# K and V loaded by quarters of the channels, and PSUM banks shared between matmuls and transposes, in a fused feed-forward and FFT-convolution kernel

## Chip, cores and metric

One core of one Trainium2 chip. The metric is the device time of one execution in microseconds (us); lower is better. A run is told with its median, lowest and highest time.

## The reference, cut to what matters

Forward and backward pass of a layer that multiplies a state-space convolution with a gated feed-forward network. B=1, S=2048 tokens, D=512 channels, F=1376, all bfloat16.

```python
def _A_ref(q, k, v, shift_k, ssm_k, ssm_D):
    k_pad = jnp.pad(k, ((0, 0), (ks - 1, 0), (0, 0)))             # ks = 4
    for t in range(ks):
        k_shift = k_shift + k_pad[:, t:t + S, :] * shift_k[:, ks - 1 - t][None, None, :]
    kv = k_shift * v
    # ... y = irfft(rfft(kv, 2S) * rfft(ssm_k, 2S))[:S], along the tokens
    y = y + kv * ssm_D[None, None, :]
    return q * y

xn = _layernorm(x)                                                # x = A_q
s  = _A_ref(xn, A_k, A_v, A_shift_k, A_ssm_k, A_ssm_D)
g  = silu((sigmoid(xn @ w_gate) * (xn @ w_up)) @ w_down)
out = x + s * g
# and jax.vjp of all this: gradients of q, k, v, shift_k, ssm_k, ssm_D and the three weights
```

## The kernel before

The kernel doesn't issue instructions as its code is run. A recorder notes every operation; a list scheduler then orders each engine's instructions by a cost model and gives each PSUM tile a bank when its first writer is placed. So all instructions carry the line of one helper (L519 here; a few lines more in kernels with code added above it), and a change of one table reorders all engines. On the chip each engine works in that fixed order and waits for semaphores.

The change touches only the first stage, the **FFT stage**, some 168 of 549 us. Four streams are woven into each other there: ten feed-forward tiles (`strG`), the transforms of the filter (`strK`), the shift convolution and the transforms of K*V (`strV`), and the products and inverse transforms (`strX`). Each of the last three goes through four quarters (`cg`) of 128 channels.

PSUM has eight banks. In the FFT stage a matmul tile takes a pair of them, a transpose tile one:

```python
KINDS = {"mm2": [(0, 1), (2, 3), (4, 5)], "mm2c": [(0, 1), (2, 3)], "mm1": [(0,), (1,), (2,), (3,)],
         "acc": [(4,), (5,)], "tr": [(6,), (7,)]}
```

K and V come in halves of 256 channels, into single buffers, on SyncE's queue. The sum of the convolution, `acc`, has a single buffer as well, and so have the filter's quarter `KT` and its spectrum `KFg`:

```python
kh_r = Ring(ar, [NJ + 3, 2 * GW])          # GW = 128 channels, NJ = 16 blocks of 128 tokens
vg_r = Ring(ar, [NJ, 2 * GW])
acc_r, term_r, kvt_r = Ring(ar, [NJ, GW]), Ring(ar, [NJ, GW]), Ring(ar, [NJ, GW])   # shortened
KFg_r = Ring(ar, [4, 1024])

def ld_k(cp):
    kh = kh_r.next()
    nc.gpsimd.memset(kh[0:1, 0:3, :], 0.0)
    nc.sync.dma_start(kh[:, 3:, :], kC[:, :, c0:c1])
    ld_halo(nc.sync, kh[:, 0:3, :], kHalo[:, 0:3, c0:c1])

def strV():                                # VectorE, quarter by quarter
    for cg in range(NG):
        acc = acc_r.next()
        for lag in (3, 2, 1, 0):           # acc = k*shift (lag 3), then term = k*shift, acc = acc + term
            ...
        nc.gpsimd.dma_start(ksh_d[cg], acc.rearrange("p j d -> p (j d)"))   # store, for the backward pass
        nc.vector.tensor_tensor(kvt, acc, vg[:, :, lc:lc + GW], ALU.mult)
        if cg == 1:
            ld_k(1); ld_v(1)               # the second half, when the single buffer is free
        ...

def strX():                                # KFg = spectrum of the filter, stored too
        for qq in range(4):
            yield from step3(QfK, qq, X_RI, KFg[:, qq])
            nc.gpsimd.dma_start(KK_d[cg, qq, :, 0], KFg[:, qq])
```

## Time and profile before

| | before |
|---|---|
| time | 550.47 us (549.67 to 550.48, 3 runs) |
| profiled span | 548.7 us |
| TensorE, VectorE, ScalarE, GpSimd busy | 526.4, 458.2, 350.6, 140.9 us |
| TensorE busy from 140 to 170 us | 27.46 of 30 us |

How to read it. A row of busy times by stage gives the stretch, its length, the busy time of TensorE, of its weight loads, of VectorE, ScalarE and GpSimd with the number of instructions, then the granted TensorE clock, the mean busy share of the 16 DMA engines, and GB/s. A timeline row gives start, length, engine, line, operation, and in brackets the idle time before it with what ended it. PE is TensorE, DVE VectorE, ACT ScalarE, POOL GpSimd, and SPq SyncE's queue, where a row's length is that of the issue and not of the transfer. A row of waits gives who waited for whom, us in total, times, longest. The lines of the kernel before that carry the argument stand in the prediction.

### The profile page before, as it was taken

How to read it: one execution, taken by the hardware profiler on the slowest of the kernel's cores; microseconds unless marked ns; L12 is line 12 of the kernel's file. 1: busy time of each engine (PE TensorE's matmuls, PEld its weight loads, DVE VectorE, ACT ScalarE, POOL GpSimd, SP SyncE). 2: the span in 40 equal slices, each digit the busy share in tenths (PEclk: the TensorE clock that was granted, in tenths of full speed). 3: DMA queues.
4: the chain of work that ended last, by engine and by line, in shares of the span. 5: the costliest groups of instructions: out<-in, count | busy, mean ns of one | idle time of the engine just before them, and what ended most of it. 6: DMA issues, size and time to landing. Idle time of an engine off the chain costs nothing.

```text
span 548.7 us, 13419 instructions
## 1 busy us (share of the span) xinstructions
PE 526.4 (96%) x5517; PEld 373.2 (68%) x5517; DVE 458.2 (84%) x831; ACT 350.6 (64%) x461; POOL 140.9 (26%) x250
## 2 busy tenths in 40 slices
PE   3999899999989999999999999999999999999996
PEld 2998798898768566677775666655666665665644
DVE  9599999956876999898989998929969999999650
ACT  7888999977985334444443345438868876966411
POOL 3225324203212222213122210221141033141221
PEclk9999999999999999999999999999999999999999
DMA  8878799857434798989999999999585469787441
GB/s 287 243 200 255 263 274 267 238 170 206 140 116 103 215 196 223 243 198 212 200 264 141 290 248 325 296 298 283 155 292 158 159 206 353 242 267 239 133 132 46
DMA packets 125287, 120.35 MB, mean 219 GB/s; under 512 B 74963, under 2 KB 104489, under 8 KB 125226
## 3 DMA queue, kind: packets, MB, share of 16 engines
q1 hardware_dynamic: 109946, 71.22, 51.9%
q0 software_dynamic: 14752, 48.27, 27.4%
q8 instruction: 43, 0.70, 0.5%
q14 instruction: 18, 0.15, 0.1%
q10 hardware_dynamic: 528, 0.00, 0.0%
HBM read 54.23 MB, written 47.55 MB: 185 GB/s over the span
## 4 chain that ended last, share of the span: by engine, by line
PE 72%; DVE 14%; issue 8%; ACT 5%; POOL 1%; POOLq 0%; ACTq 0%
PE psum L519 72%; DVE slab L519 14%; ACT slab L519 5%; POOL out_dram L519 1%; POOL slab L519 0%; POOLq L1455 0%; POOLq L519 0%; ACTq L519 0%; POOLq L1444 0%
## 5 line engine op out<-in xcount | busy, mean ns | idle before, releaser
L519 PE MATMUL psum<-slab 128*128 128x128 bf16 (+4 forms) x5517 | 526.4, 258 | 17.9 <-ACT slab L519 10.9
L519 PEld LDWEIGHTS <-slab 128*128 128x128 bf16 (+2 forms) x5517 | 373.2, 102 | 170.7 <-issue 18.7
L519 DVE TENSOR_TENSOR slab<-slab 128x512 bf16<-128x512 bf16 (+7 forms) x467 | 299.6, 683 | 7.9 <-ACT slab L519 3.0
L519 ACT CAST slab<-psum 128x1024 bf16<-128x1024 f32 (+3 forms) x252 | 207.2, 862 | 74.5 <-PE psum L519 65.9
L519 ACT COPY slab<-psum 128x1024 bf16<-128x1024 bf16 (+2 forms) x94 | 80.4, 877 | 90.1 <-PE psum L519 88.5
L519 POOL DMA_DIRECT2D out_dram<-slab x75 | 44.2, 590 | 206.8 <-ACT slab L519 111.2
L519 DVE TENSOR_TENSOR slab<-psum,slab 128x512 bf16<-128x512 f32 (+3 forms) x84 | 63.8, 760 | 23.2 <-PE psum L519 12.6
L519 ACT ACTIVATE slab<-slab 128x512 bf16<-128x512 bf16 (+3 forms) x48 | 38.6, 807 | 16.9 <-DVE slab L519 16.3
L519 ACT ACTIVATE slab<-psum 128x512 bf16<-128x512 f32 (+1 forms) x64 | 37.2, 583 | 11.5 <-PE psum L519 9.8
L519 DVE SCALAR_TENSOR_TENSOR slab<-slab 128x1 f32<-128x1 f32 (+3 forms) x64 | 27.9, 436 | 12.5 <-ACT slab L519 11.7
L519 POOL DMA_DIRECT2D KK_d<-slab x32 | 17.4, 545 | 54.7 <-ACT slab L519 43.9
L519 DVE CAST slab<-psum 128x1024 bf16<-128x1024 f32 (+1 forms) x21 | 25.1, 1196 | 5.6 <-PE psum L519 5.3
L519 POOL DMA_DIRECT2D slab<-in_A_q_dram x29 | 16.0, 552 | 30.4 <-DMA out_dram<-slab 14.9
L519 DVE COPY slab<-psum 128x1024 bf16<-128x1024 bf16 (+2 forms) x22 | 13.5, 622 | 10.9 <-PE psum L519 8.6
L519 DVE TENSOR_SCALAR slab<-slab 128x1 f32<-128x1 f32 (+7 forms) x70 | 19.5, 313 | 0.2
L519 DVE SCALAR_TENSOR_TENSOR slab<-psum,slab 128x512 f32<-128x512 f32 x16 | 11.0, 685 | 7.3 <-PE psum L519 7.2
L519 POOL TENSOR_TENSOR slab<-slab 128x1 f32<-128x1 f32 x16 | 11.5, 716 | 20.3 <-DVE slab L519 20.1
L519 POOL DMA_DIRECT2D slab<-in_grad_out_dram x16 | 8.9, 559 | 26.2 <-DMA out_dram<-slab 14.7
L519 DVE BATCH_NORM_STATS2 slab<-slab 128x6 f32<-128x512 bf16 x16 | 10.9, 681 | 0.0
L519 POOL DMA_DIRECT2D slab<-in_A_k_dram x12 | 10.1, 845 | 1.7 <-PE psum L519 1.4
L519 POOL MEMSET slab<- 1x384 bf16 (+4 forms) x14 | 5.7, 417 | 12.9 <-DVE slab L519 12.5
L519 POOL DMA_DIRECT2D slab<-slab x8 | 4.5, 567 | 10.2 <-issue 9.5
(21 smaller groups left out, 38.2 us busy)
## 6 DMA issues: line engine op xcount, KB each, us to landing
KK_d<-slab POOLq DMA_DIRECT2D x32, 256.0 KB, 3.8
slab<-KK_d SPq DMA_DIRECT2D x16, 512.0 KB, 5.6
out_dram<-slab POOLq DMA_DIRECT2D x58, 128.0 KB, 4.3
hS_d<-slab SPq DMA_DIRECT2D x16, 352.0 KB, 3.0
dgS_d<-slab SPq DMA_DIRECT2D x16, 352.0 KB, 3.4
duS_d<-slab SPq DMA_DIRECT2D x16, 352.0 KB, 4.4
slab<-hS_d SPq DMA_DIRECT2D x8, 512.0 KB, 4.8
slab<-dgS_d SPq DMA_DIRECT2D x8, 512.0 KB, 4.9
```

What stands on the lines that cost most here:

```text
L519: getattr(getattr(self.nc, eng), meth)(*[place(v) for v in a], **{x: place(v) for x, v in k.items()})
```

## The change

The intent: TensorE, 96% busy, waits now and then for the bank that its next tile needs. Matmul tiles get a fourth pair, and transposes four banks, both out of the same eight. K and V come by quarters, so that two slots let the next quarter arrive while one is worked on, and they start behind the gate weights. Their queue is GpSimd's, so that they don't block SyncE's.

```diff
-    KINDS = {"mm2": [(0, 1), (2, 3), (4, 5)], "mm2c": ...
-             "acc": [(4,), (5,)], "tr": [(6,), (7,)]}
+    KINDS = {"mm2": [(0, 1), (2, 3), (4, 5), (6, 7)], "trA": [(6,), (7,), (4,), (5,)], "mm2c": ...
+             "acc": [(4,), (5,)], "tr": [(6,), (7,)]}
...
-    PS["mm"], PS["wide"] = "mm2", True
+    PS["mm"], PS["tr"], PS["wide"] = "mm2", "trA", True
...
-    kh_r = Ring(ar, [NJ + 3, 2 * GW])
-    vg_r = Ring(ar, [NJ, 2 * GW])
+    kh_r = Ring(ar, [NJ + 3, GW], n=2)
+    vg_r = Ring(ar, [NJ, GW], n=2)
...
+    def ld_kv(cg, after=None):
+        c0, c1 = cg * GW, (cg + 1) * GW
+        kh, vg = stA["kh", cg], stA["vg", cg] = kh_r.next(), vg_r.next()
         nc.gpsimd.memset(kh[0:1, 0:3, :], 0.0)
-        nc.sync.dma_start(kh[:, 3:, :], kC[:, :, c0:c1])
+        if after is not None:                                   # holds the load back
+            nc.vector.tensor_copy(kh[0:1, 3, 0:1], after)
+            nc.vector.tensor_copy(vg[0:1, 0, 0:1], after)
+        nc.gpsimd.dma_start(kh[:, 3:, :], kC[:, :, c0:c1])
         ld_halo(nc.sync, kh[:, 0:3, :], kHalo[:, 0:3, c0:c1])
+        nc.gpsimd.dma_start(vg, vC[:, :, c0:c1])
...
-    ld_k(0)
-    ld_v(0)
+    ld_kv(0, wg[0:1, 2, 0:1])
+    ld_kv(1, wg[0:1, 2, 0:1])
...
-            if cg == 1:
-                ld_k(1)
-                ld_v(1)
+            if cg + 2 < NG:
+                ld_kv(cg + 2)
```

Cut: `ld_v`, which goes; the indices that follow from the quarters; and the return to two transpose banks after the stage.

More of the change, by code (lines that the diff above doesn't have):

```diff
@@ L188 @@
     ENGS = ("tensor", "vector", "scalar", "gpsimd", "sync")
-    KINDS = {"mm2": [(0, 1), (2, 3), (4, 5)], "mm2c": [(0, 1), (2, 3)], "mm1": [(0,), (1,), (2,), (3,)],
+    KINDS = {"mm2": [(0, 1), (2, 3), (4, 5), (6, 7)], "trA": [(6,), (7,), (4,), (5,)], "mm2c": [(0, 1), (2, 3)], "mm1": [(0,), (1,), (2,), (3,)],
              "acc": [(4,), (5,)], "tr": [(6,), (7,)]}
@@ L645, in ps_tr @@
     def ps_tr(shape, dt=bf16, name=None):
-        return nc.ps("tr", shape, dt)
+        return nc.ps(PS["tr"], shape, dt)
     ident = Ring(ar, [P]).ap
@@ L787, in ld_halo @@
         eng.dma_start(dst[113:128], src[112:127])
-    def ld_k(cp):
-        c0, c1 = cp * 256, (cp + 1) * 256
-        kh = kh_r.next()
+    def ld_kv(cg, after=None):
+        c0, c1 = cg * GW, (cg + 1) * GW
+        kh, vg = stA["kh", cg], stA["vg", cg] = kh_r.next(), vg_r.next()
         nc.gpsimd.memset(kh[0:1, 0:3, :], 0.0)
-        nc.sync.dma_start(kh[:, 3:, :], kC[:, :, c0:c1])
+        if after is not None:
+            nc.vector.tensor_copy(kh[0:1, 3, 0:1], after)
+            nc.vector.tensor_copy(vg[0:1, 0, 0:1], after)
+        nc.gpsimd.dma_start(kh[:, 3:, :], kC[:, :, c0:c1])
         ld_halo(nc.sync, kh[:, 0:3, :], kHalo[:, 0:3, c0:c1])
-        stA["kh", cp] = kh
-    def ld_v(cp):
-        vg = vg_r.next()
-        nc.sync.dma_start(vg, vC[:, :, cp * 256:(cp + 1) * 256])
-        stA["vg", cp] = vg
+        nc.gpsimd.dma_start(vg, vC[:, :, c0:c1])
     stS_r.append(Ring(ar, [FP]))
@@ L940, in strV @@
         for cg in range(NG):
-            kh, vg = stA["kh", cg // 2], stA["vg", cg // 2]
-            lc = (cg % 2) * GW
+            kh, vg = stA.pop(("kh", cg)), stA.pop(("vg", cg))
             c0, c1 = cg * GW, (cg + 1) * GW
@@ L945, in strV @@
             for lag in (3, 2, 1, 0):
-                src = kh[:, 3 - lag: 3 - lag + NJ, lc:lc + GW]
+                src = kh[:, 3 - lag: 3 - lag + NJ, :]
                 skl = skb[:, lag:lag + 1, c0:c1].to_broadcast([P, NJ, GW])
@@ L957, in strV @@
             kvt = kvt_r.next()
-            nc.vector.tensor_tensor(kvt, acc, vg[:, :, lc:lc + GW], ALU.mult)
-            if cg == 1:
-                ld_k(1)
-                ld_v(1)
+            nc.vector.tensor_tensor(kvt, acc, vg, ALU.mult)
+            if cg + 2 < NG:
+                ld_kv(cg + 2)
             yield 1024
@@ L1005, in kernel_impl @@
         r.free()
-    PS["mm"], PS["wide"] = "mm1", False
+    PS["mm"], PS["tr"], PS["wide"] = "mm1", "tr", False
     zw = {k: Ring(ar, [D], at=kv_off["kh"] + 1024 * q) for q, k in enumerate(("sigz", "gate", "s_out", "dgate", "t2"))}
```

## The prediction

> **What bounds the kernel now.** I read the page first, then the busy times by stage, then TensorE's waits and its timeline in the first 170 us (the FFT stage, which is all that the change touches), then SyncE's own timeline.
>
> The page's list of busy times, then busy time by stage (stretch, length, busy us of each engine, clock, DMA share, GB/s):
>
> ```profile
> PE 526.4 (96%) x5517; PEld 373.2 (68%) x5517; DVE 458.2 (84%) x831; ACT 350.6 (64%) x461; POOL 140.9 (26%) x250
> ...
> 0.00:15.00 15.00, 6.42 (x44) 4.75 (x45) 13.98 (x55) 11.92 (x13) 4.47 (x16) 1.00 0.85 288
> 15.00:30.00 15.00, 15.00 (x242) 14.95 (x241) 8.49 (x22) 11.70 (x17) 3.37 (x6) 1.00 0.91 225
> 30.00:110.00 80.00, 75.07 (x1118) 66.82 (x1116) 77.12 (x119) 74.38 (x94) 29.98 (x51) 1.00 0.84 251
> 110.00:140.00 30.00, 29.67 (x444) 26.42 (x442) 19.70 (x25) 23.70 (x31) 6.43 (x12) 1.00 0.62 177
> 140.00:170.00 30.00, 27.46 (x361) 22.39 (x359) 22.84 (x31) 25.80 (x30) 7.00 (x13) 1.00 0.36 118
> 170.00:549.00 379.00, 372.76 (x3323) 237.83 (x3320) 316.04 (x583) 203.11 (x281) 89.64 (x152) 1.00 0.83 221
> ```
>
> The whole is bound by TensorE: 96% busy, and its work is not changed. So the change can only give back TensorE's idle time. That is 15 - 6.4 = 8.6 us in the first 15 us, 155 - 147.2 = 7.8 us from 15 to 170 us, and 379 - 372.8 = 6.2 us in 379 us after that. From 30 to 110 us VectorE (77.1 of 80) and ScalarE (74.4 of 80), which empty PSUM, are as full as TensorE. There is little to win there by buffers alone.
>
> TensorE's waits from 0 to 170 us (us in total, times, longest), then its timeline at the start and at the end of that stage (start, length; idle before in brackets):
>
> ```profile
> PE psum L519 <- ACT slab L519: 10.0, 16, 4.2
> PE psum L519 <- DVE slab L519: 3.0, 5, 1.9
> PE psum L519 <- DMA slab<-in_A_shift_k_dram: 2.2, 1, 2.2
> ```
>
> ```profile
> 8.28 1.89 PE L519 MATMUL psum<-slab 128*128 128x128 bf16 x16 [4.18 <-ACT slab L519]
> 12.09 1.86 PE L519 MATMUL psum<-slab 128*128 128x128 bf16 x16 [1.92 <-DVE slab L519]
> 14.20 22.78 PE L519 MATMUL psum<-slab 128*128 128x128 bf16 x368 [0.25 <-ACT slab L519]
> ...
> 157.32 3.97 PE L519 MATMUL psum<-slab 128*128 128x128 bf16 x52 [0.46 <-DVE slab L519]
> 162.41 5.27 PE L519 MATMUL psum<-slab 128*128 128x512 bf16 x59 [1.12 <-ACT slab L519]
> 168.08 2.11 PE L519 MATMUL psum<-slab 128*128 128x128 bf16 x35 [0.40 <-ACT slab L519]
> ```
>
> No wait of TensorE after 2.2 us is for a DMA. All are for an engine that empties PSUM or makes an operand. A matmul is shown 0.22 us long though the next starts 0.0555 us after it, so short stalls hide in the busy time. Taking starts instead (step to the next matmul less 0.0555 us, or less 0.214 us for 512 columns, where more than 0.05 us is over), I count 13.7 us of stalls from 15 to 170 us. When I follow the kernel's built order, in nearly every one the operand had long been there, and the matmul came just after the eviction of the tile that held its PSUM bank before. With 2.7 us such in the first 15 us, bank waits make 16.4 us.
>
> SyncE's timeline, the loads of K (512-byte runs), V and the filter:
>
> ```profile
> 5.59 8.41 SPq L519 DMA_DIRECT2D slab<-in_A_k_dram  x2
> 14.04 0.55 SPq L519 DMA_DIRECT2D slab<-in_A_v_dram  x1
> 14.72 3.64 SPq L519 DMA_DIRECT2D slab<-in_A_ssm_k_dram  x1
> ...
> 60.44 0.57 SPq L519 DMA_DIRECT2D slab<-in_A_k_dram  x1
> 64.30 0.56 SPq L519 DMA_DIRECT2D slab<-in_A_v_dram  x1
> ```
>
> K blocks the queue from 5.6 to 14.0 us, but the weights were issued ahead of it and land by 13.5 us; the filter's second quarter lands only at 24.8 us. The second half of K and V is asked for at 60 us, when its single buffer is free, and lands at 66.9 and 75.6 us; TensorE uses it at 96.8 us. Nobody waits for it.
>
> **What the Trainium skill says.** "Perfetto Trace Analysis", Optimization Strategy: the same gap repeating on the engine that should be saturated can mean there isn't enough PSUM for the next tile. The 21 waits above agree. "TensorE: Matmul & The Clock Gate", Part 1: a cold array starts 128-column matmuls every 107 ns, a warm one every 56 ns. Here the 16 transposes at 12.09 us come 107 ns apart, and those after about 18 us 55.5 ns, so work that starts earlier also warms the array earlier. "DMA: Bandwidth & Descriptors", Issuing engines are not separate DMA queues: moving a load to GpSimd saves the issuing queue's time only. The same page, Specifications, wants 512 bytes or more per run; the quarters have 256. A K quarter of this form, loaded by GpSimd at 408.87 us late in this trace, landed 5.3 us after its issue with 1.2 us of issue. That is slower per byte, but no disaster.
>
> **The change part by part.**
>
> *PSUM.* In the FFT stage matmuls may use four bank pairs, not three; transposes four single banks, not two. The number of banks stays eight, so this is flexibility, not capacity. The order of the changed kernel can be read before it runs. For each PSUM tile I added up the TensorE work (0.0555 or 0.214 us each) between the last matmul of the bank's former tile and its own first, and summed what falls short of 1.3 us (an eviction of 1024 columns takes 1.0 us on ScalarE, 1.2 on VectorE, plus a matmul's 0.2). Before: 15.0 us, after 11.5. That is an index, not a time, but the 15.0 stand against 16.4 us measured, so -3.5 of index is some -3.8 us. By place: first 8 us of TensorE work 3.9 to 5.0; to 24 us 0.8 to 0.1; 24 to 95 us 8.3 to 8.4; the last 42 us 5.5 to 2.9. So the gain should be at the end of the stage, some 2 us, and hardly any (I put 0.7, for the earlier start of what follows) where VectorE and ScalarE are full.
>
> *The head.* At 12.09 us the first filter transposes waited 1.92 us for a bank that VectorE emptied late. Their operand was ready at 10.44 us. With four transpose banks they start near 10.6 us, are 107 ns apart, and one of the two evictions moves from ScalarE to VectorE; so the first FFT matmuls, at 14.58 us before, come at about 13.3 us: -1.3 us. The index rises there because later work moves up behind it.
>
> *K and V.* Four tiny copies of about 0.15 us on VectorE, 0.6 us in the first 13 us, hold K and V back until half of the gate weights has landed (9.6 us before), which is earlier than VectorE gets to the copies: no wait. GpSimd issues four loads of 1.2 us from about 12.4 to 17.2 us. At some 2.5 us of data each they should be in by 27 us; the shift convolution began at 31.55 us. The filter quarter now goes from SyncE at about 12.5 us and lands near 17-20 us instead of 24.8; its transposes are placed about 10 us of TensorE work earlier, at roughly 20 us. Worth by itself: nothing, 0 to -0.5 us, as no wait was for K or V.
>
> Sum: -1.3 - 0.7 - 2.0 = -4.0 us; 550.5 - 4.0 = 546.5 us.
>
> **Rivals.** (1) *VectorE and ScalarE are the true bound of the stage.* For it: 96 and 93% from 30 to 110 us, 22.8 and 25.8 of 30 from 140 to 170 us. Then a freed bank only moves the wait and all that remains is the head: 548.5 to 549.5 us. (2) *New waits from the loads.* The filter's transposes now stand before the end of the first feed-forward tile; if the filter shares the DMA engines with 2 MB of short runs and lands after 20 us, TensorE waits for it in order. Also a layer-norm step on GpSimd stands behind the four issues, until about 17.5 us, used near 20 us. Either could cost 1 to 4 us: 548 to 552 us. (3) *Sharing hurts:* one transpose in bank 6 or 4 blocks a whole pair. The built order has this in it, and the index doesn't rise past the head. (4) *More than counted:* all 16.4 us of bank waits can't go, since evictions take their time; half of them would be 542 us.
>
> **Range and chances.** Middle 546.5; (4) sets the low end at 542.5, (1) and (2) the high end at 550.0. For 2% faster (539.5) nearly all recorded idle time of the stage except the start would have to go: 4%. For 2% slower, 11 us of new waits: 2%. Within 2%: 94%.
>
> **What would show it.** Right: TensorE's second group of transposes starts near 10.6 us and the long unbroken group near 13; idle from 15 to 170 us falls from 7.8 to some 5-6 us, mostly after 140 us; busy times of all engines stay; no TensorE wait for a DMA after 15 us; after 170 us the same 6 us idle. Wrong: a wait of TensorE or VectorE for K, V or the filter between 15 and 45 us; idle unchanged after 140 us (rival 1); or a change after 170 us, where I expect none.

## More of the kernel before

A finished feed-forward tile is transposed by the DMA, from SBUF to SBUF, and then stored; both go through SyncE's queue:

```python
nc.sync.dma_start_transpose(st.rearrange("p (a b) -> p a b", b=128), srcT.rearrange("p a t -> p (a t)"))
...
nc.sync.dma_start(dst, st)                 # hS_d
```

One more view matters later: SyncE's own timeline of the kernel before, around the DMA transpose of the second feed-forward tile.

```profile
40.01 1.43 SPq L519 DMA_TRANSPOSE slab<-slab  x1
44.04 0.34 SPq L519 DMA_DIRECT2D hS_d<-slab  x1
```

The store of the transposed tile goes out 4 us after the transpose, as soon as that is done. In the same stretch the store of the first convolution's sum (`ksh_d`) landed 6.1 us after its issue at 42.9 us.

## The result, and the profile after

The changed kernel took 548.12 us (547.8 to 548.75, 4 runs) beside 550.24 us of the kernel before in the same rounds: a ratio of 0.9964 [0.9947, 0.9982]. Ratios in this document are the mean time of one kernel's fast runs over that of the other's of the same rounds, with a 95% interval, so not quite the ratio of the medians quoted. Executions over 1.5% slower than the fastest of the same kernel are left out of the means. The kernel was run once more, in another session, beside three experiments:

> The changed kernel once more, unaltered, beside the three that follow, on their chip. Expected: 547.5 to 549.0 us, 0.995 to 0.9975 of the kernel before, mean clock 1.0 in the profiled run. If it comes out at 1.000 or above, the gain of 2 us measured first was a matter of one session and there is nothing to explain.

It gave 548.15 us (548.02 to 548.78), ratio 0.9967 [0.9953, 0.9980]. The 2 us are real, and half of the 4 us foretold. The trace of this second session is complete (the first lacks 59 matmul records) and is used from here on; where both have a step, they agree within 0.1 us. Its page's line of busy times and its busy time by stage:

```profile
PE 524.3 (96%) x5517; PEld 371.5 (68%) x5517; DVE 457.3 (84%) x841; ACT 347.1 (63%) x455; POOL 150.6 (28%) x260
...
0.00:15.00 15.00, 7.81 (x67) 5.90 (x68) 13.73 (x58) 12.30 (x13) 6.73 (x19) 1.00 0.84 278
15.00:30.00 15.00, 13.47 (x229) 13.10 (x227) 9.38 (x28) 12.29 (x17) 7.96 (x11) 1.00 1.07 256
30.00:110.00 80.00, 73.04 (x1089) 64.96 (x1087) 75.15 (x114) 70.46 (x88) 32.45 (x54) 1.00 0.90 242
110.00:140.00 30.00, 29.64 (x436) 26.03 (x434) 20.47 (x28) 23.55 (x28) 6.78 (x13) 1.00 0.67 189
140.00:170.00 30.00, 29.41 (x412) 24.88 (x412) 24.72 (x42) 26.76 (x34) 7.84 (x15) 1.00 0.41 135
```

TensorE gains 1.4 us of busy time in the first 15 us (6.42 to 7.81) and 1.95 us in the last stretch (27.46 to 29.41). It loses 1.5 us from 15 to 30 us and 2.0 us from 30 to 110 us, where the prediction saw a small gain. TensorE's timeline at the start, and GpSimd's:

```profile
10.51 3.90 PE L519 MATMUL psum<-slab 128*128 128x128 bf16 x44 [0.29 <-DVE slab L519]
14.84 1.09 PE L519 MATMUL psum<-slab 128*128 128x128 bf16 x16 [0.43 <-ACT slab L519]
16.24 3.45 PE L519 MATMUL psum<-slab 128*128 128x128 bf16 x59 [0.31 <-ACT slab L519]
20.17 1.63 PE L519 MATMUL psum<-slab 128*128 128x128 bf16 x25 [0.47 <-ACT slab L519]
22.55 2.66 PE L519 MATMUL psum<-slab 128*128 128x128 bf16 x43 [0.75 <-ACT slab L519]
```

```profile
12.74 1.20 POOL L519 DMA_DIRECT2D slab<-in_A_k_dram  x1
13.93 2.27 POOL L519 DMA_DIRECT2D slab<-in_A_v_dram  x1
16.19 1.15 POOL L519 DMA_DIRECT2D slab<-in_A_k_dram  x1
17.33 1.15 POOL L519 DMA_DIRECT2D slab<-in_A_v_dram  x1
18.50 0.57 POOL L519 TENSOR_TENSOR slab<-slab 128x1 f32<-128x1 f32 x1
```

The 1.9 us wait at 12.09 us is gone; the transposes start at 10.51 us. But a step of a layer norm on GpSimd (18.50 us) now stands behind the four issues, and VectorE waits 2.4 us for it. That is passed on to ScalarE and comes back to TensorE as the waits at 20.17 and 22.55 us.

**The lead.** To see where time is won or lost, I counted TensorE's work in its built order (each matmul at the distance of back-to-back starts, 0.0557 us, or 0.2147 us for 512 columns) and compared when each kernel had done the same amount. Negative: ahead of the kernel before, in us, at the moment when that one stood at the time in the head row.

| kernel | 25 us | 61 us | 93 us | 142 us | 199 us |
|---|---|---|---|---|---|
| changed kernel | -0.5 | -2.7 | +2.1 | +1.6 | -2.5 |
| banks alone | -2.0 | -2.3 | +4.8 | +5.0 | +1.6 |
| loads alone | -0.8 | -0.3 | -0.1 | +0.6 | +1.0 |
| second half's loads late | -0.5 | -2.6 | +5.9 | +6.0 | +2.6 |
| second quarter later | -2.2 | 0.0 | +3.9 | +3.3 | -0.8 |
| changed, two sums | -0.6 | -2.8 | +1.2 | +0.8 | -3.3 |
| second quarter later, two sums | -2.2 | -4.3 | +2.5 | +2.0 | -2.1 |
| banks alone, two sums | -1.8 | -3.7 | +2.6 | +2.9 | -0.6 |
| second quarter later, plain copies | -2.2 | -4.3 | -0.1 | -0.6 | -4.7 |
| pairs shared, transposes in two banks | -0.8 | -1.5 | +1.4 | +1.4 | -0.5 |

The kernels are those of the experiments below. From 199 us to 297 us, the last point compared, the curves are flat: the rest of the program only starts earlier or later (only the one with the second half's loads late loses 3.2 us more). The profiled spans differ by 1.7 us (548.7 and 547.0) where the lead is 2.5 us; where the other 0.8 us goes was not followed (at 540 us the lead is still 2.3 us, so most of it goes at the very end). The changed kernel's tale is: 2.4 us ahead at 16 us, 1.9 given back, 2.2 more won by 61 us, 4.7 lost by 93 us, 4.1 won after 142 us.

### The profile page after: what moved, and what is told of

It is laid out like the page before. It is cut to its first block, busy times and chain, and to the rows that moved or that the text cites. A ratio compares the mean times of both kernels' runs of the same rounds, so it can differ in the third digit from the quotient of the medians.

```text
span 546.9 us, 13392 instructions
## 1 busy us (share of the span) xinstructions
PE 520.3 (95%) x5458; PEld 371.5 (68%) x5517; DVE 457.2 (84%) x841; ACT 347.1 (63%) x455; POOL 151.0 (28%) x260
## 4 chain that ended last, share of the span: by engine, by line
PE 66%; DVE 16%; issue 8%; ACT 5%; POOL 2%; DMA 1%; POOLq 0%; DVEq 0%; ACTq 0%
PE psum L519 66%; DVE slab L519 16%; ACT slab L519 5%; DMA ksh_d<-slab 1%; POOL out_dram L519 1%; POOL slab L519 1%; ACT L519 0%; POOLq L1451 0%; POOL KK_d L519 0%; POOLq L519 0%; DVEq L519 0%; ACTq L519 0%; POOLq L1440 0%
## 5 line engine op out<-in xcount | busy, mean ns | idle before, releaser
L519 PE MATMUL psum<-slab 128*128 128x128 bf16 (+3 forms) x5458 | 520.3, 256 | 21.7 <-ACT slab L519 11.5
L519 ACT CAST slab<-psum 128x1024 bf16<-128x1024 f32 (+4 forms) x260 | 214.2, 866 | 80.2 <-PE psum L519 72.4
L519 ACT COPY slab<-psum 128x1024 bf16<-128x1024 bf16 (+2 forms) x82 | 68.5, 861 | 85.5 <-PE psum L519 85.2
L519 ACT ACTIVATE slab<-slab 128x512 bf16<-128x512 bf16 (+3 forms) x46 | 36.8, 805 | 18.4 <-DVE slab L519 17.8
L519 DVE COPY slab<-psum 128x1024 bf16<-128x1024 bf16 (+2 forms) x34 | 21.0, 636 | 8.1 <-PE psum L519 7.8
L519 DVE CAST slab<-psum 128x1024 bf16<-128x1024 f32 (+1 forms) x13 | 14.8, 1141 | 4.7 <-PE psum L519 4.5
L519 POOL DMA_DIRECT2D slab<-in_A_k_dram x16 | 14.9, 930 | 7.1 <-DVE slab L519 3.9
L519 POOL TENSOR_TENSOR slab<-slab 128x1 f32<-128x1 f32 x16 | 10.6, 663 | 13.6 <-DVE slab L519 13.3
L519 POOL DMA_DIRECT2D slab<-sF_d x7 | 3.8, 537 | 22.7 <-DVE slab L519 18.5
L519 POOL MEMSET slab<- 1x384 bf16 (+3 forms) x16 | 5.9, 376 | 14.5 <-DVE slab L519 11.3
```

Of the source, the lines that this page charges most:

```text
L519: getattr(getattr(self.nc, eng), meth)(*[place(v) for v in a], **{x: place(v) for x, v in k.items()})
```

## The experiments

Each diff below is against the changed kernel unless said otherwise. Results were correct except where "wrong" stands.

### 1. The banks alone, and the loads alone

The first kernel has only the changes of `KINDS` and `PS`, the second only those of the loads.

> The kernel before with the PSUM part of the change alone (four bank pairs for matmuls, four single banks for transposes; K and V as before). Theory A (the gain is the banks', and the new loads cost in the middle of the stage, because they let VectorE take up the convolutions of quarters 2 and 3 early): 2.5 to 4 us faster than before (ratio 0.993 to 0.9955), that is, at least as fast as the full change at 0.9964. Theory B (the gain is the loads'): within 0.5 us of before. In the trace, A: first FFT matmuls near 13.2 us as in the full change, and no loss against before from 58 to 95 us.

> The changed kernel with the old PSUM banks (three pairs, two single): the loads of K and V alone. Theory A: 0 to 2 us slower than before (ratio 1.000 to 1.004). Theory B: about 2 us faster (0.9964). Both: the first transposes of the filter wait for a bank until about 12.1 us as before, so the head is not won.

Measured: banks alone 551.63 us (549.3 to 552.03), ratio 1.0007 [0.9989, 1.0026]; loads alone 552.51 us (551.88 to 553.12), 1.0041 [1.0029, 1.0053]. The theory that the loads make the gain falls, but so does the simple form of its rival: neither part gains anything alone.

The table of the lead tells more than the times. The head belongs to the banks: alone they are 2.0 us ahead at 25 us, and nothing takes it back, since no K/V issues stand before the layer norm. The end belongs to the banks too: -3.4 us from 142 to 199 us with the banks alone, +0.4 with the loads alone. What spoils the banks alone is the middle. VectorE's timeline there:

```profile
51.31 2.48 DVE L519 TENSOR_TENSOR slab<-slab 128x2048 bf16<-128x2048 bf16 x2 [5.08 <-DMA ksh_d<-slab]
```

The second convolution may not write `acc` before the first one's sum has been read out by the store. The store landed at 51.3 us, and VectorE, which works in order, stood for 5.1 us. In the changed kernel the same wait is 0.4 us; in the kernel before there is none.

The table shows one thing more. From 61 to 93 us every kernel with shared banks loses 2.9 to 8.5 us, the loads alone 0.2. So the loss in the middle goes with the sharing, or with the order that it brings, even where no store is late.

### 2. When K and V are asked for

Two kernels with the banks shared. In the first, quarters 2 and 3 are asked for together after the second convolution, as before; in the second, quarter 1 waits for the last constant of the FFT.

```diff
-            if cg + 2 < NG:
-                ld_kv(cg + 2)
+            if cg == 1:
+                ld_kv(2, acc[0:1, 0, 0:1])
+                ld_kv(3, acc[0:1, 0, 0:1])
```

> The changed kernel, but quarters 2 and 3 of K and V are held until the convolution of quarter 1 is done, about 66 us, as before (a tiny copy from its result gates them). If the early convolutions of quarters 2 and 3 cost the 4.7 us that the changed kernel loses against before from 58 to 95 us, this one loses at most 2 there and ends 1.5 to 3 us faster than the full change (ratio to before 0.991 to 0.994). If that loss has another cause (bank sharing, order by chance), it ends within 0.7 us of the full change (0.995 to 0.998).

```diff
-    ld_kv(1, wg[0:1, 2, 0:1])
...
+    ld_kv(1, R[0:1, 3, 0, 0, 1:2])        # after the constants are made
```

> The changed kernel, but the loads of quarter 1 are gated on the last constant that VectorE makes (about 15.5 us), so that the layer-norm step of the second tile on GpSimd no longer stands behind four load issues. TensorE's order is the same as in the full change. If the 1.8 us that the changed kernel gives back between 14 and 25 us come from that step (at 19 us there, 15.7 us before), the wait of the transposes at 20.2 us for it goes (0.6 us) and the following one at 22.6 us (0.9 us) shrinks; TensorE is 1 to 1.5 us earlier at 25 us. If evictions bound the middle, most of it is absorbed by 100 us and the total is within 0.5 us of the full change (0.9955 to 0.9975); else it ends 1 us or more faster (0.993 to 0.9947).

Measured: 556.29 us (551.28 to 557.45), 1.0095 [1.0066, 1.0124], and 551.42 us (548.4 to 552.02), 1.001 [0.9991, 1.0029]. The first expectation failed outright. The second held for the head (2.2 us ahead at 25 us where the changed kernel has 0.5, so the queue of issues before the layer norm did cost about 1.7 us) and failed for the end time: a lead of 3.5 us at 53 us was gone at 61 us. The views of that second kernel: SyncE's timeline, busy times by stage, and the timelines of VectorE and TensorE.

```profile
40.17 4.02 SPq L519 DMA_TRANSPOSE slab<-slab  x1
55.27 0.36 SPq L519 DMA_DIRECT2D hS_d<-slab  x1
```

```profile
45.00:50.00 5.00, 4.69 (x75) 4.46 (x73) 4.27 (x9) 4.72 (x7) 1.96 (x4) 1.00 1.28 78
...
56.00:64.00 8.00, 5.94 (x60) 5.77 (x60) 8.00 (x9) 3.40 (x4) 1.69 (x4) 0.57 0.81 290
```

```profile
53.67 2.96 DVE L519 TENSOR_TENSOR slab<-slab 128x2048 bf16<-128x2048 bf16 x3 [3.10 <-DMA ksh_d<-slab]
```

```profile
57.81 3.57 PE L519 MATMUL psum<-slab 128*128 128x128 bf16 x32 [3.31 <-DVE slab L519]
```

In the kernel before, the second of these stretches was:

```profile
45.00:50.00 5.00, 4.38 (x70) 3.90 (x68) 4.41 (x10) 4.45 (x6) 2.79 (x5) 1.00 1.00 363
```

Read from the top: a DMA transpose issued at 40.17 us is followed by its store only at 55.27 us, 15 us later, against 4 us in the kernel before. Meanwhile the DMA engines are shown fully busy (1.28), yet move 78 GB/s (363 before). The `ksh_d` store in GpSimd's queue lands 12.3 us after its issue (6.1 before). VectorE stands for it 3.1 us. TensorE then stands for VectorE 3.3 us, from 54.5 to 57.8 us, and meanwhile its **clock is halved**: the granted clock is 0.57 on average from 56 to 64 us. The trace has it at 0.5 from 56.61 to 63.44 us. The banks alone have 3.41 us of it, from 63.56 us, and the first of these two kernels 3.41 us, from 85.42 us, after a DMA transpose that was issued at 63.79 us with its store leaving at 83.42 us. The kernel before and the changed one, once they have full clock (at 17.6 and 13.0 us), have none until their last matmul is over.

The Trainium skill, "TensorE: Matmul & The Clock Gate", table in Why this matters for your kernels, tells to leave no idle gaps over some 3 us, since one idle window puts the clock back to half. The trace agrees: the stalls were 3.3 us (second kernel here) and 5.0 us (first). But the window needn't be idle. In these traces the clock changes in steps of 3.413 us. Counting each matmul that starts in such a window at the distance of back-to-back starts, as for the lead, the array's use was 0.26, 0.10 and 0.31 in the windows ahead of the three half-clock stretches (second kernel here, first, banks alone). Windows at full clock with 0.36, 0.40 and 0.45 (in the kernels of experiment 3) were followed by no half clock, and none of the fourteen traces has an exception.

So there was a new theory (C): a late store stops VectorE or ScalarE at a single buffer, these stop TensorE, and the clock gate doubles the price. The rival (D): the wait only marks the place, and the lead would be lost anyway.

### 3. Two buffers for the sum

Three kernels get a second `acc`. To change nothing else, the recorder sees the old addresses; only when instructions are emitted are those of odd quarters moved to the second buffer. So the order on every engine is exactly that of the kernel it is made from (compared instruction by instruction), and only the wait is gone. The second buffer is the one of K*V, which moves to the last quarter of `y2A`, not yet in use.

```diff
-            acc = acc_r.next()
+            acc = ar.view(acc_r.blks[0][0], [NJ, GW], bf16)
+            if cg % 2:
+                nc.moved[id(acc)] = (acc, kvt_r.ap)             # address used at emission
...
+            # every view of kvt: emitted as the view of y2A[:, :, 3 * GW:4 * GW]
```

> The changed kernel with two buffers for the sum of the shift convolution, used in turn; every engine has exactly the instructions and the order of the changed kernel, only the wait of a convolution for the store of the sum before it is gone. (The second buffer is the one of the product K*V, which moves to the last quarter of y2A, unused at that time.) Theory C (a VectorE that stands in order behind a late ksh_d store holds TensorE and halves its clock): in the changed kernel this wait is 0.6 us in one place and the clock isn't lowered, so little is to be had: 547.0 to 548.5 us, 0.9945 to 0.997. Rival D (the time between 58 and 95 us goes to something else, such as banks or the place of other work): the same as the changed kernel. This run is the control of the next two: it must not differ from the changed kernel by more than 1 us.

> The kernel with the loads of the second quarter issued later (551.42 us), with two buffers for the sum; every engine's instructions and order are those of that kernel. Theory C: the wait of VectorE for the store (3.1 us), TensorE's stall of 3.5 us at 57.8 us and the 6.8 us at half clock that follow it go, and the lead of 3.5 us that this kernel had at 52 us stays: 545.5 to 548.0 us, 0.991 to 0.996, mean clock 1.0, faster than the changed kernel. Rival D (the wait only marks the place, the lead is lost to other things): 550 to 552 us, and the low clock stays.

> The kernel with the shared PSUM banks alone (551.63 us), with two buffers for the sum; every engine's instructions and order are those of that kernel. Theory C: the wait of 5.1 us for the store and the 3.4 us at half clock go, and what the banks are worth by themselves appears: 547.0 to 549.5 us, 0.9935 to 0.999, mean clock 1.0. Rival D (the banks alone gain nothing, with or without that wait): 550.5 to 552 us, 1.0005 to 1.003, whatever the clock does.

Measured: changed kernel 548.06 us (547.94 to 549.51), 0.9969 [0.9957, 0.9982], as expected of a control. Second quarter later: 548.89 us (median of six; five fast runs from 546.24 to 552.72, and one of 554.9, which the ratio leaves out), 0.9975 [0.9940, 1.0009]. Banks alone: 550.0 us (548.61 to 553.93), 1.0018 [0.9987, 1.0049].

The chain is as theory C has it: no wait for `ksh_d`, no lowered clock in the stage, and at 61 us the leads are 4.3 and 3.7 us where they had been 0.0 and 2.3. But the expected end times were missed (the banks alone gained nothing clear: 1.0018, and 1.0007 with one sum). By the traces the **next single buffer** caught the lateness. Second quarter later, ScalarE's timeline; and banks alone, VectorE's waits (us, times, longest):

```profile
63.16 1.93 ACT L520 CAST slab<-psum 128x1024 bf16<-128x1024 f32 x2 [3.65 <-DMA KK_d<-slab]
```

```profile
DVE slab L520 <- DMA slab<-in_A_ssm_k_dram: 2.6, 1, 2.6
```

ScalarE now waits for the store of `KFg`, VectorE for the load of the filter's last quarter. The fast runs scatter by 5 to 6.5 us, those with the longest times at a mean clock of 0.996 or 0.997. So the buffer isn't the root. The lateness of transfers is.

### 4. Without DMA transposes

The kernel with the second quarter later (one `acc`), with the FFT stage's DMA transposes emitted as plain copies of the same tiles in the same place of the same queue. The stored h is wrong on purpose.

```diff
+                if op.n in self.plain:                          # the transposes of the FFT stage
+                    meth, a = "dma_start", (a[0].rearrange("p a b -> p (a b)"), a[1])
```

> The kernel with the loads of the second quarter issued later (551.42 us; ksh_d store issued at 41 us and landed at 53.6 us; 6.8 us at half clock), where the DMA transposes of the FFT stage are emitted as plain copies of the same tiles, in the same place of the same queue. The stored h is wrong on purpose, everything else is as it was. Theory C (the store lands late because a DMA transpose and the transfers of GpSimd's queue slow each other down): the store lands by 50.5 us, VectorE waits under 0.5 us for it, no half clock, 545.5 to 548.5 us. Rival G (GpSimd's queue is late by its own load, the transposes don't matter): the store lands after 52.5 us as before, the low clock stays, 550 to 552 us.

Measured: 547.12 us (546.49 to 547.71), 0.9942 [0.9925, 0.9958]. SyncE's timeline and busy times by stage:

```profile
37.58 0.47 SPq L522 DMA_DIRECT2D slab<-slab  x1
40.42 0.36 SPq L522 DMA_DIRECT2D hS_d<-slab  x1
```

```profile
45.00:50.00 5.00, 4.64 (x75) 4.45 (x74) 4.27 (x10) 4.71 (x7) 1.95 (x4) 1.00 1.02 352
```

With the same loads and stores, 352 GB/s flow where 78 did. The `ksh_d` store lands at 49.1 us, not 53.6. VectorE doesn't wait for it, the clock stays full, and the lead is 4.3 us at 61 us and 4.7 at the end. It is the lowest median of all, with the old single buffer, and 4.3 us below the kernel that it differs from by these copies alone (0.9942 and 1.001 of the kernel before, in two sessions: 3.7 us by these ratios). No kernel with correct results beat the changed one beyond the scatter. This confirms, for this kernel, that the late stores come from DMA transposes in flight beside the transfers of GpSimd's queue. For the banks alone and the kernel with the second half's loads late, where a transpose takes 11.0 and 19.6 us to its store, only the traces speak for it. The packets of both slow down: from 45 to 50 us those of the transpose (256 bytes) took 89 ns on average, where the kernel before has 22 ns (40 to 45 us), and those of GpSimd's queue (4096 bytes) 683 ns, where 193 ns do with plain copies. Why, no trace here shows. Whether they meet is a matter of a few us: in the changed kernel the transpose is issued at 39.23 us, its store leaves at 45.70 us, and it does little harm.

### 5. VectorE in the middle

Even without late stores a lead of 2.8 us at 61 us turns into +1.2 at 93 us (changed kernel with two sums). VectorE is busy 34.4 of 35 us from 60 to 95 us there. Is it the bound (theory E)? Both kernels with two sums, with 12 VectorE instructions left out at emission (wrong), in the same order otherwise:

```diff
+                    if cg > 0 and lag > 0:                      # lags 2 and 1 of quarters 1 to 3
+                        nc.skip.update((o1.n, o2.n))            # the multiplication and the addition
```

> The changed kernel with two sum buffers (548.06 us) with 12 VectorE instructions left out, in the same order otherwise: the terms of lags 2 and 1 (a multiplication and an addition each, about 1.05 us) in the convolutions of quarters 1 to 3. The result is wrong on purpose. Theory E (VectorE, 97 to 98% busy between 30 and 95 us in both kernels, sets the pace there, so that TensorE can't keep a lead through it, whatever banks it has): with 12.6 us less of VectorE work TensorE keeps its lead, its busy time between 60 and 95 us rises from 31.2 to over 33.5 us; 542.0 to 545.0 us. Rival F (the lead is lost to waits for PSUM banks, transfers or the order itself): 546.5 to 548.5 us. It is to be read beside the next run: under E the changed kernel is then faster than before by 4 to 6.5 us, under F by 1 to 3 us as it is now.

> The kernel before with two sum buffers and the same 12 VectorE instructions left out (wrong on purpose too). It is the reference for the run above. Theory E: before has fewer banks and a TensorE that already ran 95% of the time between 60 and 95 us, so it gains less: 547.0 to 549.5 us. Rival F: the same gain as in the changed kernel, so that their distance stays 1 to 3 us.

Measured: changed 547.46 us (547.28 to 551.4), 0.9958 [0.9933, 0.9982]; before 549.42 us (548.71 to 550.13), 0.9979 [0.9963, 0.9996]. The distance of the medians is 2.0 us, as it was (1.2 us by the ratios, in which the run of 551.4 us counts). Busy time by stage of the changed one, first with the full work of VectorE, then with these left out:

```profile
60.00:95.00 35.00, 31.20 (x471) 27.88 (x468) 34.36 (x53) 31.67 (x40) 13.60 (x21) 1.00 0.92 234
```

```profile
60.00:95.00 35.00, 31.30 (x477) 28.48 (x479) 23.80 (x41) 31.94 (x41) 12.35 (x20) 1.00 0.82 229
```

VectorE fell from 34.4 to 23.8 us, TensorE stayed at 31.2 to 31.3. Theory E is refuted: a unit busy 98% of a stretch was not what held the others there. TensorE still waits for ScalarE (2.7 us from 60 to 95 us in the view of waits) more than for VectorE (0.8), and ScalarE is busy 31.9 of 35 us. Which engine empties which tile is fixed by the order, so VectorE's free time couldn't help. Whether ScalarE or the order itself sets the pace was not tried.

Where the time goes can be read, though. The built order tells which tile held a bank before. Over the work that the kernel before does from 61 to 93 us, TensorE's stalls by starts are 2.5 us there, all at matmul tiles. In the changed kernel (one sum) the same work has 7.2 us: 4.5 at matmul tiles and 2.6 at transpose tiles, whose banks ScalarE had emptied; 1.1 of these 2.6 us are in banks that a matmul tile had held.

### 6. Which half of the bank sharing

Matmuls keep the fourth pair, transposes go back to banks 6 and 7.

```diff
-... "trA": [(6,), (7,), (4,), (5,)]
+... "trA": [(6,), (7,)]
```

> The changed kernel with the fourth pair of banks for matmuls, but the transposes of the FFT stage kept to banks 6 and 7. The order changes with it, so its middle may fall either way by 2 us. Theory H (the end of the stage gains by the fourth matmul pair, the head by the transposes' four banks): TensorE is busy 29.0 us or more between 140 and 170 us, as after, but its wait of 1.9 us at 12 us is back; 547.5 to 550 us. Rival I (the transposes' banks make the end of the stage): TensorE is busy 27.5 us there as before, 550.5 to 552.5 us.

Measured: 551.16 us (550.27 to 555.59), 1.0024 [0.9995, 1.0053]. Busy time by stage:

```profile
0.00:15.00 15.00, 6.41 (x44) 4.71 (x45) 13.82 (x59) 12.46 (x13) 6.75 (x19) 1.00 0.83 274
...
140.00:170.00 30.00, 28.44 (x394) 24.01 (x396) 22.08 (x33) 28.08 (x34) 7.55 (x14) 1.00 0.42 136
```

The head is back at 6.41 us of TensorE work, as before (6.42): it needs the transposes' four banks. At the end of the stage 28.44 us lie midway between 27.46 before and 29.41 after: both halves of the sharing have a part. Neither theory was right as stated: the time missed the first one's by more than 1 us and came out where the second had it.

## Why the prediction was right, and where it was not

The total was right in range, 548.1 us against 546.5 in 542.5 to 550.0; of the 4.0 us foretold 2.0 came. The gain's kind, TensorE's waits for banks at the head and the end of the stage, was right. That the total still came out in range was partly luck: the end won 4.1 us where 2.0 were foretold, which made up for a middle that lost 2.1 and a head of which 0.5 stayed. By its steps:

- **The head, -1.3 us: right in mechanism, then given back.** The transposes start at 10.51 us (foretold 10.6) and the first FFT matmuls at 13.13 us (13.3). The lead reached 2.4 us at 16 us: 1.45 us from this earlier start, the rest from the clock, which is full from 13.0 us instead of 17.6. (The prediction says that an earlier start warms the array earlier, but doesn't count it. In all ten traces whose transposes start at 10.5 us the full clock comes between 11.7 and 14.4 us, in the four others between 15.8 and 17.6.) Then rival 2, the layer-norm step behind the four issues, took 1.9 us; the prediction named it with the right engine, a microsecond early, but left it out of its sum. Experiment 1 shows the gain with the banks alone, experiment 2 shows that it stays if the issues come later.
- **The middle, -0.7 us: the step that failed.** The prediction put "hardly any" gain there. The net from 25 to 142 us is a loss of 2.1 us. Its index of bank shortage, 8.3 before and 8.4 after for this stretch, takes 1.3 us for every eviction and says nothing of when the evictions really come: TensorE's waits from 30 to 95 us, counted by starts, grew from 7.9 to 10.2 us. (The index has a slip too: its four places add up to 18.5 before and 16.4 after, not to the 15.0 and 11.5 given as totals. The forecast's sum doesn't use these.) A lead won before such a stretch isn't kept.
- **The end, "some 2 us": right in place and cause, mis-sized.** From 142 to 199 us 4.1 us were won; waits by starts from 140 to 170 us fell from 4.0 to 1.3 us. All kernels with four shared pairs and four transpose banks win 3.4 to 4.1 us there, and the loads alone lose 0.4.
- **K and V, "nothing, 0 to -0.5 us": half right.** The first two quarters landed by 28 us (27 foretold), and no engine waited for one of their loads. That the loads are worth something only through what they do to other transfers was not seen. With the loads as before, shared banks meet the late store, for which VectorE stands 5.1 us; with the new ones they happen to miss it (0.4 us), which is luck, not foresight. By themselves the new loads cost 2.2 us.
- **Rival 1** (VectorE and ScalarE are the bound) was right that the middle gives nothing, wrong on VectorE by experiment 5, and wrong that only the head would remain: the end won. **Rival 3** (sharing hurts) is not refuted: the middle's loss goes with the shared banks, although in the stretch counted in experiment 5 it was transposes that waited for a matmul tile's bank (1.1 us) and not the reverse. **Rival 4** didn't come.
- **The marks.** "Idle from 15 to 170 us falls to some 5-6 us" was wrong: 155 less 145.6 us of busy time is 9.4 us, up from 7.8, although it fell from 2.5 to 0.6 us after 140 us as said. The long unbroken group near 13 us didn't come; four waits break it up to 22.6 us. The first trace puts one of them, 0.3 us at 16.3 us, down to the filter's load, a mark of being wrong; the second puts the same wait down to ScalarE. Busy times of all engines stayed but for GpSimd's (140.9 to 150.6 us). After 170 us the lead still grows by 0.8 us, then it stands at 2.5 us from 199 us to the last point compared, 297 us.

What stays open: what sets TensorE's pace between 60 and 95 us (ScalarE, the sharing or the order that it brings), and why DMA transposes and GpSimd's transfers slow each other down.

## What to carry to other kernels

Follow a gain through the whole program: a lead on the bounding engine counts only if the stages after it keep it, and a comparison at equal work shows where it is won and lost when the total hides it. When a part of a change gains nothing alone, look for a wait that appears only in its order; single buffers behind a store are where a transfer's lateness turns into a stall, and a second buffer may only move the stall to the next one. An engine that is 98% busy is not thereby the bound: take work off it before believing so.

## What the Trainium skill lacked or had wrong

- "DMA: Bandwidth & Descriptors", Rules for kernel authors, where it tells which DMA transposes to serialize, says that one next to ordinary DMAs needs nothing. That holds for results, which were right in every run not made wrong, but not for time: beside GpSimd's loads and stores a transpose of 352 KB took 15 us until its store could go (4 us in the kernel before) and 78 GB/s moved in all, against 352 with plain copies in its place.
- "TensorE: Matmul & The Clock Gate", Part 1: The HAM clock gate, gives idle and busy windows but no threshold between them. Here windows at full clock with 0.31 or less of the array's time in use led to half clock, those with 0.36 and more did not.
- No page gives a figure for how long issuing loads of short runs holds up other work on GpSimd. Here the issues of K and V quarters (256-byte runs) took 1.15 to 2.27 us each, 5.8 us for four, with a computation of 0.57 us in the same instruction stream behind them.
